# Softmax attention with a gated MLP on one core: head quads outside, chunks inside, VectorE exponentials as four shifted bit lines, one shifted add on GpSimd

## Chip, cores, metric

One core of one Trainium2 chip. The metric is device time in microseconds (us) of one execution. On one core the state of a run (fast or slow) is judged only by its time against other runs of the same kernel. Ratios below are of fast runs, made on the same chip side by side with the kernel before; times are medians of all runs. Experiments of different rounds ran on different chips, on which the kernel before took 1037.57 to 1041.86 us. "Quarter" means 512 of the 2048 columns of one batch; a "batch" is one key block of 128 keys for four heads and 512 queries, exponentiated on VectorE.

## The reference

```python
x = A_x                                    # 1 x 2048 x 640, bf16
g = sigmoid((x * gate_w).sum(-1, keepdims=True))
q, k, v = split(x @ wqkv)                  # 32 heads of 20 dimensions
p = softmax(q @ k.T * 20 ** -0.5)          # 2048 x 2048 for each head
a = (p @ v) @ wo
h = x @ w1 + b1                            # 640 -> 1536
b = (h * tanh(log1p(exp(-|h|)) + max(h, 0))) @ w2
return g * a + (1 - g) * b
```

There are 32 x 2048 x 2048 exponentials. They are the heavy part: 32 groups (four heads by 512 queries), each with 16 key blocks.

## The kernel before

A scheduler written in Python lays all work in one fixed order per engine when the program is built. It uses assumed costs (in ns); each engine is then given its instructions in that order. TensorE computes scores into PSUM, ScalarE exponentiates 13 of 16 key blocks in tiles of 1536 and 1024 columns, VectorE the other three, and TensorE multiplies by V ("PV"), accumulating a group in one PSUM bank, `C`. VectorE's exponential writes integers whose bits, read as bf16, are close to an exponential (a "bit line"), and mends it with a mantissa polynomial:

```python
DVE_KEYS = (6, 10, 14)                  # the other 13 key blocks are ScalarE's
...
def p1(r=r, db=db, vb_=vb_):            # one bit line of 512 columns, from PSUM
    nc.vector.tensor_scalar(out=vb_.tile[:, r * QC:(r + 1) * QC], in0=db.tile[:, :],
        scalar1=P * LOG2E * inv, scalar2=127.0 * P, op0=ALU.mult, op1=ALU.add)
...
# then, for 4 heads x 512 columns: two bit operations (n, m) of 2048 columns,
# two squares and two products of 1024 columns each, all on VectorE
pv_four(G, j, 1, sl(vb_), list(p1s), [vb_], key=G)      # three PV sets a key block
pv_four(G, j, 0, sl(nb_), [tn], [nb_], key=G)
pv_four(G, j, 2, sl(mb_), tp_, [mb_], key=G)
```

A PV set is four matmuls, one for each head, each on 32 of the 128 columns of the array. The projections (K, Q, MLP, output) are whole 128-column matmuls, put between. GpSimd only clears and pads buffers at the start.

The softmax here doesn't subtract the row's maximum and nothing guards it: scores larger than these inputs give would overflow.

Of the kernel before, what the change touches and what calls it, by code (L numbers as in the profile page):

```python
# [2 lines left out]

# [9 lines left out]
ENG = mybir.EngineType  # L13
# [9 lines left out]
VW = 22  # L23
NO = 12


DVE_KEYS = (6, 10, 14)
ACT_KEYS = tuple(j for j in range(NS) if j not in DVE_KEYS)



COEF = (0.458054, 0.465699, 0.0762946)
SCALE = 0.5 / COEF[1]
COEF = tuple(SCALE * c for c in COEF)
LOG2E = 1.4426950408889634


class Task:
    __slots__ = (
        "eng", "cost", "fn", "deps", "after", "prio", "ring", "need", "frees",  # L40
        "start", "end", "lat", "mode", "rows", "n", "key", "left", "succ",
    )

    def __init__(self, eng, cost, fn, deps=(), after=None, prio=5, ring=None,
                 frees=(), lat=70, mode=None, rows=(), key=0):
        self.eng, self.cost, self.fn = eng, cost, fn
        self.deps, self.after, self.prio = [d for d in deps if d], after, prio
        self.ring, self.frees = ring, list(frees)
        self.lat, self.mode, self.rows, self.key = lat, mode, rows, key
        self.start = self.end = None  # L50


class Ring:
    def __init__(self, *slots):
        self.free = deque((0.0, s) for s in slots)

    def when(self):
        return self.free[0][0] if self.free else None


class Buf:


    def __init__(self, ring):
        self.ring, self.users, self.tile, self.last, self.slot = ring, 0, None, 0.0, None


class Order:


    SWITCH = 60.0
# [10 lines left out]

    def run(self):
        now = {}
        mode = None
        rows = set()
        open_ = {}
        waiting = {}
        for i, t in enumerate(self.tasks):
            t.n = i  # L90
            t.succ = []
            t.left = 0
        for t in self.tasks:
            for d in set(t.deps + ([t.after] if t.after else [])):
                d.succ.append(t)
                t.left += 1
            open_.setdefault(t.eng, [])
            now.setdefault(t.eng, 0.0)
            if t.left == 0:
                open_[t.eng].append(t)  # L100
        done = 0
        out = []
        self.rowheld = 0

        def est(t):
            e = now[t.eng]
            for d in t.deps:
                ready = d.end + (d.lat if d.eng != t.eng else 0 if t.eng == "PE" else 40)
                if ready > e:
                    e = ready  # L110
            if t.after and t.after.start > e:
                e = t.after.start
            if t.ring:
                w = t.ring.ring.when()
                if w is None:
                    return None
                e = max(e, w + 70)
            return e

        def cost(t):  # L120
            if t.eng != "PE":
                return t.cost
            c = t.cost
            if t.mode != mode:
                c += self.SWITCH
            elif t.mode == "row" and not (rows & set(t.rows)):
                c = 40
            return c

        while done < len(self.tasks):  # L130
            best = None
            for eng, lst in open_.items():
                c = [(est(t), t) for t in lst]
                c = [(e, t) for e, t in c if e is not None]
                if not c:
                    continue
                first = min(e for e, _ in c)
                pick = None
                if eng == "PE":
                    hot = [(e, t) for e, t in c if t.prio == 0]  # L140
                    lim, ht = min(hot, key=lambda x: x[0], default=(1e12, None))
                    slack = 0 if ht is None else 350 if len(ht.rows) == 3 else 750
                    here = [(e, t) for e, t in c if e <= first + 1]
                    if any(t.mode == "row" and t.prio == 1 for _, t in c) and not self.rowheld:
                        here = [
                            (e, t) for e, t in here
                            if not (t.ring and t.prio > 1 and len(t.ring.ring.free) < 2)
                        ]
                    here.sort(key=lambda x: (x[1].prio, x[1].key, x[1].n))
                    for e, t in here:  # L150
                        if t.mode == "row" and t.prio == 1 and lim < 1e12 and not (
                            mode == "row" and not (rows & set(t.rows))
                        ):
                            continue
                        if t.prio == 0 or e + cost(t) <= lim + slack:
                            pick = (e, t)
                            break
                    if pick is None:
                        pick = min(hot or c, key=lambda x: x[0])
                    if mode == "row" and pick[1].prio != 0:  # L160
                        for e, t in here:
                            if t.mode == "row" and t.prio == 1 and not (rows & set(t.rows)):
                                pick = (e, t)
                                break
                else:
                    here = [(e, t) for e, t in c if e <= first + 20]
                    pick = min(here, key=lambda x: (x[1].prio, x[1].key, x[1].n))
# [3 lines left out]
            c = cost(t)  # L171
            if t.eng == "PE":
                if t.mode == "row" and mode == "row" and not (rows & set(t.rows)):
                    rows |= set(t.rows)
                else:
                    rows = set(t.rows)
                mode = t.mode
            t.start, t.end = e, e + c
            now[t.eng] = t.start + (60 if t.eng == "SP" else c)
            open_[t.eng].remove(t)  # L180
            if t.mode == "row" and t.prio == 1:
                self.rowheld += 1
            if t.ring:
                t.ring.slot = t.ring.ring.free.popleft()[1]
            if t.eng == "DVE" and t.prio == 1 and t.rows:
                self.rowheld -= 1
            for b in t.frees:
                b.users -= 1
                b.last = max(b.last, t.end)
                if b.users == 0:  # L190
                    f = b.ring.free
                    f.append((b.last, b.slot))
                    b.ring.free = deque(sorted(f))
            for s in t.succ:
                s.left -= 1
                if s.left == 0:
                    open_[s.eng].append(s)
            done += 1
# [5 lines left out]
ORDER = []  # L204


def vcost(n, per=1.04, base=160):
    return base + per * n
# [3 lines left out]
def kernel(  # L212
# [11 lines left out]
):  # L224
    nc = tc.nc
# [3 lines left out]
    use_dve = len(DVE_KEYS) > 0  # L229
    NA, ND = len(ACT_KEYS), len(DVE_KEYS)  # L230

    const = ctx.enter_context(tc.tile_pool(name="const", bufs=1))
    ident = const.tile([P, P], BF16, tag="ident")
    kt_all = const.tile([P, NP, S], BF16, tag="kt_all")
    xt = const.tile([P, NQ, KT, QC], BF16, tag="xt")
    va = const.tile([P, NA * H * VW + 16], BF16, tag="va")
    vd = const.tile([P, max(1, 3 * ND) * H * VW + 16], BF16, tag="vd", name="vd")
    wq = const.tile([P, NP, KT, P], BF16, tag="wq")
    wo = const.tile([P, NP, D], BF16, tag="wo")
    w1 = const.tile([P, KT, F], BF16, tag="w1")  # L240
    w2k = const.tile([P, 5120 + KT * 641 + 3], BF16, tag="w2k")
# [4 lines left out]
    z = const.tile([P, NS], F32, tag="z")  # L246
    lnc = const.tile([P, 1], F32, tag="lnc")
    arena = const.tile([P, 18432], BF16, tag="arena")

    w2 = w2k[:, 0:FT * D].rearrange("p (f c) -> p f c", c=D)  # L250
    wk = w2k[:, 0:NP * KT * P].rearrange("p (q k c) -> p q k c", q=NP, k=KT)
    wv = w2k[:, 5120:5120 + KT * 641].rearrange("p (k c) -> p k c", c=641)
    xs = arena[:, 0:NS * D].rearrange("p (s c) -> p s c", c=D)
    wqk = arena[:, 10240:10240 + KT * 2 * D].rearrange("p (k c) -> p k c", c=2 * D)
    hs = arena[:, 0:FT * QC].rearrange("p (f q) -> p f q", q=QC)
    tanh_in = arena[:, 6144:6144 + FT * QC].rearrange("p (f q) -> p f q", q=QC)
    outs = arena[:, 6144:6144 + NU * D].rearrange("p (u c) -> p u c", c=D)
    otn = arena[:, 12288:12288 + NO * QC].rearrange("p (h q) -> p h q", q=QC)
    bs = xt[:, 0].rearrange("p k q -> p (k q)").rearrange("p (u c) -> p u c", c=D)

    psum = ctx.enter_context(tc.tile_pool(name="psum", bufs=1, space=bass.MemoryType.PSUM))
    epool = ctx.enter_context(tc.tile_pool(name="epool", bufs=3))
    vpool = ctx.enter_context(tc.tile_pool(name="vpool", bufs=2))
    qpool = ctx.enter_context(tc.tile_pool(name="qpool", bufs=3))
    opool = ctx.enter_context(tc.tile_pool(name="opool", bufs=1))
    spool = ctx.enter_context(tc.tile_pool(name="spool", bufs=2))
# [4 lines left out]
    R = {  # L271
        "S3": Ring(0), "S2": Ring(0), "X": Ring(0, 1), "E3": Ring(0, 1, 2), "E2": Ring(0, 1),
# [568 lines left out]
```

## Time and profile before

1043.57 us (median of 3, 1031.25 to 1044.37).

| what | before |
|---|---|
| span of the profiled run | 1038.2 us |
| ScalarE (ACT) busy | 921.6 us, 89% |
| TensorE (PE) busy | 831.3 us, 80% |
| VectorE (DVE) busy | 790.8 us, 76% |
| GpSimd (POOL) busy | 35.3 us, 3% |
| mean granted TensorE clock | 0.859 |

The page's first part of the kernel before: busy us of each engine, its share of the span, instructions. Then the first line of the page's fourth part: the chain of work that ended last, shares of the span.

```profile
PE 831.3 (80%) x6247; PEld 267.3 (26%) x6304; DVE 790.8 (76%) x1322; ACT 921.6 (89%) x731; POOL 35.3 (3%) x29
...
ACT 49%; PE 28%; issue 11%; DVE 7%; DMA 4%; SPq 1%; ACTq 0%; DVEq 0%
```

ScalarE is the busiest engine and holds half of the chain: it is what the change must relieve.

Groups of instructions by shape, of the kernel before. Columns: line, engine, operation, out<-in, shapes, count | busy us, mean ns of one | idle us of the engine before them and who ended it.

```profile
L597 ACT ACTIVATE E<-S,lnc 128x1536 bf16<-128x1536 f32 x333 | 523.0, 1571 | 27.7 <-PE S L579 19.3 <-PE X L634 8.2
L597 ACT ACTIVATE E<-S,lnc 128x1024 bf16<-128x1024 f32 x332 | 379.9, 1144 | 44.8 <-PE C L507 41.9 <-PE X L634 1.5 <-PE S L579 0.6
...
L646 DVE TENSOR_SCALAR e<-X 128x512 uint16<-128x512 f32 x384 | 260.8, 687 | 135.7 <-PE X L634 131.8 <-PE S L579 1.1
...
L653 DVE TENSOR_SCALAR n<-e 128x2048 uint16<-128x2048 uint16 x96 | 65.8, 685 | 0.0
...
L328 POOL COPY wq<-arena 128x400 bf16<-128x400 bf16 x7 | 3.4, 523 | 0.0
```

The last line is one of two alike, the only elementwise work for which GpSimd reads a tile in this trace, apart from one 0.3 us instruction that builds the identity matrix: a bf16 copy of 400 columns. Remember it. No line shows GpSimd adding to a uint16 tile.

Two stretches of the table of stretches, kernel before (us from the start: length, then busy us and instruction count of each engine, then the granted TensorE clock, DMA share and GB/s):

```profile
416.00:442.00 26.00, 25.47 (x220) 9.73 (x220) 23.47 (x41) 25.48 (x21) 0.00 (x0) 1.00 0.09 31
...
494.00:520.00 26.00, 16.05 (x103) 4.30 (x105) 18.68 (x28) 24.31 (x18) 0.00 (x0) 0.75 0.05 11
```

ScalarE (the fourth busy figure) is near 26 of 26 us in both. In the first TensorE was busy for 25.47 us and its clock was 1.00; in the second for 16.05 us, at 0.75.

### The profile page before, as it was taken

The numbers are of one execution on the slowest core, as the hardware profiler recorded it, in microseconds if no ns is written. First come the engines' busy times: TensorE is split into PE (matmuls) and PEld (weight loads), VectorE is DVE, ScalarE is ACT, GpSimd is POOL, SyncE is SP. The second block draws the span as 40 slices with busy tenths as digits, with TensorE's granted clock in tenths as the row PEclk, the third lists the DMA queues.
The fourth block names the chain that finished last, engine by engine and source line by source line (L and its number), as shares of the span: only waits on it lengthen the run. The fifth ranks groups of instructions, "written<-read, shape, count | busy, mean of one in ns | idle before, by whom it ended". The sixth has DMA issues, their size and how long they took to land.

```text
span 1038.2 us, 15472 instructions
## 1 busy us (share of the span) xinstructions
PE 831.3 (80%) x6247; PEld 267.3 (26%) x6304; DVE 790.8 (76%) x1322; ACT 921.6 (89%) x731; POOL 35.3 (3%) x29
## 2 busy tenths in 40 slices
PE   2899988887886589996689889667988967798885
PEld 1432222221121123321123322112322311132213
DVE  1698989887784769995679879677888975689772
ACT  1757879998999999999999999999999999999991
POOL 9300000000000000000000000000000000000000
PEclk9998999886696779997789989787989997599766
DMA  7400000011000000000000000000000000000001
GB/s 196 109 1 12 12 11 11 12 55 36 9 12 11 11 1 12 25 24 12 11 1 12 18 25 18 12 12 1 12 12 25 24 12 11 1 12 12 11 11 37
DMA packets 28495, 22.36 MB, mean 22 GB/s; under 512 B 15496, under 2 KB 23688, under 8 KB 28424
## 3 DMA queue, kind: packets, MB, share of 16 engines
q1 hardware_dynamic: 24744, 19.15, 6.7%
q10 hardware_dynamic: 3680, 2.23, 0.8%
q8 instruction: 49, 0.80, 0.3%
q14 instruction: 22, 0.18, 0.1%
HBM read 18.22 MB, written 2.88 MB: 20 GB/s over the span
## 4 chain that ended last, share of the span: by engine, by line
ACT 49%; PE 28%; issue 11%; DVE 7%; DMA 4%; SPq 1%; ACTq 0%; DVEq 0%
ACT E L597 40%; PE S L579 8%; PE C L507 7%; ACT arena L745 6%; PE X L763 3%; PE X L778 3%; PE X L427 2%; DVE e L646 2%; ACT L745 2%; PE X L439 2%; DMA rbc<-rows 2%; PE X L462 2%; PE X L727 1%; DMA w2k<-in_A_wqkv_dram 1%; ACT L597 1%
## 5 line engine op out<-in xcount | busy, mean ns | idle before, releaser
L597 ACT ACTIVATE E<-S,lnc 128x1536 bf16<-128x1536 f32 (+1 forms) x666 | 822.4, 1357 | 72.5 <-PE C L507 41.9
L579 PE MATMUL S<-q,kt_all 32*128 32x512 bf16 x1664 | 290.5, 428 | 146.1 <-ACT E L597 139.7
L646 DVE TENSOR_SCALAR e<-X 128x512 uint16<-128x512 f32 x384 | 260.8, 687 | 135.7 <-PE X L634 131.8
L507 PE MATMUL C<-E,va 128*32 128x512 bf16 x1664 | 183.3, 438 | 2.7 <-DVE oraw L690 1.5
L579 PEld LDWEIGHTS <-kt_all 32*128 32x128 bf16 x1664 | 83.4, 92 | 382.7 <-issue 375.6
L634 PE MATMUL X<-q,kt_all 32*128 32x512 bf16 x384 | 156.1, 428 | 3.6 <-DVE e L646 3.3
L663 DVE TENSOR_TENSOR m<-m 128x1024 bf16<-128x1024 bf16 x192 | 127.2, 683 | 0.3
L668 DVE TENSOR_TENSOR m<-m,e 128x1024 bf16<-128x1024 bf16 x192 | 126.6, 681 | 0.0
L507 PEld LDWEIGHTS <-va 128*32 128x32 bf16 x1664 | 42.5, 95 | 129.4 <-issue 127.4
L727 PE MATMUL X<-xt,w 128*128 128x512 bf16 x219 | 70.5, 416 | 2.5 <-issue 1.7
L658 DVE TENSOR_SCALAR m<-e 128x2048 uint16<-128x2048 uint16 x96 | 66.2, 690 | 6.6 <-PE C L507 4.0
L763 PE MATMUL X<-w2k,arena 128*128 128x320 bf16 x384 | 69.6, 305 | 0.7 <-DVE e L646 0.7
L745 ACT ACTIVATE arena<-arena 128x2048 bf16<-128x2048 bf16 x36 | 68.2, 1917 | 0.2
L653 DVE TENSOR_SCALAR n<-e 128x2048 uint16<-128x2048 uint16 x96 | 65.8, 685 | 0.0
L778 PE MATMUL X<-wo,arena 128*128 128x320 bf16 x256 | 49.3, 325 | 7.8 <-DVE arena L717 6.5
L507 PE MATMUL C<-e,vd 128*32 128x512 bf16 x384 | 49.5, 442 | 4.1 <-DVE e L646 2.2
L507 PE MATMUL C<-m,vd 128*32 128x512 bf16 x384 | 49.1, 452 | 4.2 <-DVE m L668 4.2
L439 PE MATMUL X<-xt,wq 128*128 128x512 bf16 x137 | 48.6, 446 | 2.3 <-issue 1.8
L733 DVE TENSOR_SCALAR arena<-X,b 128x512 bf16<-128x512 f32 x48 | 35.8, 746 | 18.7 <-PE X L727 18.5
L507 PEld LDWEIGHTS <-vd 128*32 128x32 bf16 x1152 | 34.6, 99 | 57.7 <-issue 51.6
L507 PE MATMUL C<-n,vd 128*32 128x512 bf16 x384 | 42.7, 432 | 5.7 <-DVE n L653 5.5
L427 PE MATMUL X<-xt,w2k 128*128 128x512 bf16 x147 | 44.2, 403 | 2.4 <-issue 1.1
(55 smaller groups left out, 435.7 us busy)
## 6 DMA issues: line engine op xcount, KB each, us to landing
rbc<-rows SPq DMA_DIRECT2D x128, 64.0 KB
out_dram<-arena SPq DMA_DIRECT2D x16, 160.0 KB
w<-in_B_w_dram SPq DMA_DIRECT2D x1, 1920.0 KB
w2k<-in_B_w_dram SPq DMA_DIRECT2D x1, 1920.0 KB
arena<-in_A_wqkv_dram SPq DMA_DIRECT2D x2, 700.0 KB
arena<-in_A_x_dram ACTq DMA_DIRECT2D x2, 640.0 KB
arena<-in_A_x_dram SPq DMA_DIRECT2D x2, 640.0 KB
wo<-in_A_wo_dram SPq DMA_DIRECT2D x4, 200.0 KB
```

What stands on the lines that cost most here:

```text
L439: nc.tensor.matmul(t[:, 0:QC], lhsT=wq[:, p, k, :], rhs=xt[:, qc, k, :], start=a, stop=b)
L507: nc.tensor.matmul(acc[32 * r:32 * r + 32, :], lhsT=ten[:, off:off + 32], rhs=srcs[r](), start=k == 0, stop=k == pv_per - 1, tile_position ...
L579: nc.tensor.matmul(sb.tile[:, a * QC:(a + 1) * QC], lhsT=kt_all[32 * r:32 * r + 32, G % NP, j * P:(j + 1) * P], rhs=q_buf[G].tile[32 * r:3 ...
L597: nc.scalar.activation(eb.tile[:, 0:w], sb.tile[:, 0:w], ACT.Exp, bias=lnc, scale=inv)
L634: nc.tensor.matmul(db.tile[:, :], lhsT=kt_all[32 * r:32 * r + 32, G % NP, j * P:(j + 1) * P], rhs=q_buf[G].tile[32 * r:32 * r + 32, :], st ...
L646: nc.vector.tensor_scalar(out=vb_.tile[:, r * QC:(r + 1) * QC], in0=db.tile[:, :], scalar1=P * LOG2E * inv, scalar2=127.0 * P, op0=ALU.mul ...
L663: nc.vector.tensor_tensor(out=m, in0=m, in1=m, op=ALU.mult)
L668: nc.vector.tensor_tensor(out=m, in0=m, in1=e, op=ALU.mult)
L727: nc.tensor.matmul(t[:, 0:QC], lhsT=w1[:, k, ft * P:(ft + 1) * P], rhs=xt[:, c, k, :], start=a, stop=b)
L745: nc.scalar.activation(v, hs[:, 4 * a:4 * a + 4, :] if func == ACT.Exp else v, func, bias=1.0 if func == ACT.Ln else 0.0)
L763: nc.tensor.matmul(t[:, 0:320], lhsT=hs[:, k, u * P:(u + 1) * P], rhs=w2[:, k, 320 * hf:320 * hf + 320], start=a, stop=b)
L778: nc.tensor.matmul(t[:, 0:320], lhsT=otn[:, (c * NP + k) % NO, u * P:(u + 1) * P], rhs=wo[:, k, 320 * hf:320 * hf + 320], start=a, stop=b)
```

## The change

Intent: take more exponentials off ScalarE and make VectorE's cheaper. Four of 16 key blocks go to VectorE. Each is now a sum of four bit lines: the first is made from PSUM as before, three are the same integers plus 19, 51 and 90; the sum is made by PV's accumulation, so a key block has four PV sets instead of three and no polynomial. Two of the three shifted adds are VectorE's, the third is GpSimd's, in quarters. The loops are turned round: four heads outside, the four query chunks inside, so K and V are projected a bit at a time through the whole run. The projections (V's excepted) become four 32-column matmuls ("column-tiled"), so that TensorE need not change mode between them and PV. The mode is the way the array is divided for a matmul: whole, in strips of columns or in strips of rows; the scheduler reckons 100 ns for a change. Mish loads fewer activation tables (9 loads instead of 25).

The core of the diff:

```diff
-DVE_KEYS = (6, 10, 14)
-COEF = (0.458054, 0.465699, 0.0762946)
+SHIFTS = (0, 19, 51, 90)
+SUM = 5.2566
+def dve_keys(G):
+    n = 4
+    return [int((i + 0.4) * NS / n) for i in range(n)]
+TB = (2, 2, 1, 1)                      # buffers of each line's tile
+SHIFT_ON = {1: ("DVE", 1), 2: ("DVE", 1), 3: ("POOL", 4)}
 ...
+    def columns(t, width, lhsT, rhs, a, b):
+        for r in range(4):
+            nc.tensor.matmul(t[32 * r:32 * r + 32, 0:width], lhsT=lhsT(r), rhs=rhs,
+                             start=a, stop=b, tile_position=(0, 32 * r))
 ...
-            # bit operations n, m; squares; products (VectorE)
+        for i in range(1, len(SHIFTS)):
+            eng, parts = SHIFT_ON[i]
+            now = []
+            for a in range(parts):
+                def add(i=i, eng=eng, a=a, w=4 * QC // parts):
+                    ...
+                    (nc.vector if eng == "DVE" else nc.gpsimd).tensor_scalar(
+                        out=bufs[i].tile[:, a * w:(a + 1) * w],
+                        in0=bufs[0].tile[:, a * w:(a + 1) * w],
+                        scalar1=float(SHIFTS[i]), scalar2=None, op0=ALU.add)
+                n = 4 * QC // parts
+                now.append(o.add(eng, 150 + 0.264 * n if eng == "DVE" else 160 + 1.0 * n, add,
+                                 p1s[...] + now[-1:], prio=3, ...,
+                                 rings=[bufs[i]] if a == 0 else [], frees=[bufs[0]], port=True))
 ...
-        qc, p = divmod(G, NP)
+        p, qc = divmod(G, NQ)
```

(Cut: the scheduler's rewritten choice rules, new loads, the placing of the normalized output.) Note the assumed cost of a GpSimd quarter, `160 + 1.0 * n` = 672 ns, and `port=True`: the scheduler plans VectorE's shifted adds and GpSimd's quarters as excluding each other.

## The prediction

> **Bound now: ScalarE.** The page's first part has ACT busy 921.6 us of 1038.2 (89%), PE 831 (80%), DVE 791 (76%), GpSimd 35. In the chain of waits ACT's exponential line holds 40%. By the table of stretches ACT runs at about 97% from 286 to 1014 us. Its 117 us of idle time: 27 us before the first exponential, 24 us after the last, about 30 us between 52 and 156 us, where the K and V projections of all heads crowd.
>
> **ScalarE after.** VectorE takes four of 16 key blocks instead of three: 1536 exponential blocks for 1664, 307 pairs (1536 and 1024 wide) for 332.5. Their union is 834 us for 665, 2.51 us a pair (neighbours overlap): -64 us. The new instruction order has 9 activation table loads for 25, each 1.28 us: up to -20 us. ACT busy about 850 us.
>
> **VectorE after.** Out: 192 bit operations (0.69 us), 384 half-tile multiplies (0.68 us), threefold V copies: about -400 us. In: 128 more bit lines from PSUM (0.69 us, +88) and 256 shifted adds of 2048 columns (estimate 0.69 us, as the bit operations: +177). In all about 735 us. GpSimd gets 512 quarter adds; its copy of 400 columns took 524 ns, so I estimate 0.67 us each, 345 us. The Trainium skill, "SBUF — State Buffer", section "Who interferes with whom", says that a DVE instruction in a 2-port mode and a GpSimd instruction exclude each other for a whole instruction; the trace before has no such overlap. I allow 30 to 60 us of lengthened adds: DVE busy 765 to 795 us.
>
> **TensorE after.** PV goes from 22 to 28 sets of four matmuls per group (+192 x 0.21 = +41 us at full clock); output projection 8 to 6 steps (-9 us). Projections become four column-tiled matmuls, which cost one slot as PV fours do (0.21 to 0.23 us apart in the timeline) and need no mode change against PV: in the instruction order mode changes fall from about 1500 to 1250, at about 0.1 us (-25 us). TensorE's work stays equal within 10 us. Stretches with denser PE had clock 1.00, the thinner Mish ones 0.72 to 0.83; spread work should hold 0.85 to 0.95.
>
> **Head quads outside** spreads K and V projections over the run: most of the 30 us of early idle time goes. The start loads less before the first exponential (27 us to about 20). The tail gains a placing DMA but loses matmul time: about 24 us again.
>
> **Sum.** ACT 850 + start 20 + tail 25 + inner idle 30 to 60 (DVE gets denser) = 925 to 955. Predicted 938 us, range 905 to 985. Chances: faster by over 2% 0.92, within 2% 0.06, slower 0.02.
>
> **What would show it.** ACT busy 840 to 865 and leader of the chain; 615 exponentials; 9 table loads; DVE 765 to 795, shifted adds over 0.69 us on average; GpSimd 320 to 400; no ACT stretch after 60 us under 90%; PE busy share 80 to 88%.
>
> **What would make it wrong.** GpSimd's quarters much longer than 0.67 us, so that the lock makes DVE the bound (over 88% busy) and ScalarE waits for PE, PE for VectorE's bit lines; column-tiled projections of 320 columns over 0.14 us a slot because four weight loads do not hide; a lower TensorE clock: towards 985 or beyond. A start and steady stretch without gaps: towards 905.

## The result and the profile after

1111.22 us (median of 4, 1106.65 to 1114.51) against 1041.86 us: the ratio of the fast runs is 1.068, 95% interval 1.060 to 1.077. (Ratios here and below are the mean time of one kernel's fast runs over that of the other's in the same rounds, so not quite the ratio of the quoted medians.) The change is slower by 7%, outside the range and on the wrong side.

The same two parts of the page, of the changed kernel:

```profile
PE 945.5 (85%) x10616; PEld 307.2 (28%) x10616; DVE 721.5 (65%) x1097; ACT 853.1 (77%) x663; POOL 837.1 (75%) x519
...
PE 42%; POOL 38%; DVE 7%; ACT 7%; issue 5%; DMA 1%; SPq 0%; DVEq 0%; ACTq 0%; POOLq 0%
```

ScalarE did fall to the 850 us that were predicted, yet the run got longer: it is now idle for 257 us (1110.2 - 853.1). GpSimd is busy for 837 us instead of the predicted 345, and holds 38% of the chain.

Groups by shape, changed kernel:

```profile
L674 POOL TENSOR_SCALAR t<-t 128x512 uint16<-128x512 uint16 x512 | 831.5, 1643 | 244.5 <-PE C L588 123.0 <-DVE t L661 117.3 <-PE X L407 3.7
L627 ACT ACTIVATE E<-S,lnc 128x1536 bf16<-128x1536 f32 x307 | 473.7, 1543 | 176.8 <-PE C L588 113.1 <-PE X L600 34.2 <-PE S L600 27.0
...
L674 DVE TENSOR_SCALAR t<-t 128x2048 uint16<-128x2048 uint16 x256 | 211.2, 833 | 11.3 <-PE C L588 9.3
```

A quarter takes 1643 ns on average, 2.4 times what the scheduler assumed and I estimated. The query of that source line gives the spread (min/median/max ns, first and last start in us):

```profile
L674 POOL TENSOR_SCALAR t<-t x512: 1482/1490/2467, 17.8 to 1080.5; 128x512 uint16<-128x512 uint16 x171
L674 DVE TENSOR_SCALAR t<-t x256: 629/738/1148, 22.5 to 1081.0; 128x2048 uint16<-128x2048 uint16 x128
```

The minimum and the median are alike: 1.49 us is what the instruction costs when nothing disturbs it. The 0.15 us up to the mean are taking turns with VectorE (experiment 6, where they vanish).

Who waited for whom, changed kernel (us in total, times, longest us):

```profile
ACT E L627 <- PE C L588: 133.8, 113, 6.4
...
POOL t L674 <- PE C L588: 123.0, 108, 9.4
POOL t L674 <- DVE t L661: 117.3, 87, 11.7
...
PE C L588 <- POOL t L674: 85.0, 98, 2.0
```

And how this looks in time: the timeline of the changed kernel, GpSimd's, ScalarE's and some of TensorE's rows of PV on bit lines.

```profile
524.39 6.84 POOL L674 TENSOR_SCALAR t<-t 128x512 uint16<-128x512 uint16 x4 [2.13 <-PE C L588]
...
528.94 0.39 PE L588 MATMUL C<-t,va 128*32 128x512 bf16 x2
...
529.83 0.38 PE L588 MATMUL C<-t,va 128*32 128x512 bf16 x1 [0.50 <-POOL t L674]
...
531.28 0.38 PE L588 MATMUL C<-t,va 128*32 128x512 bf16 x1 [1.08 <-POOL t L674]
...
531.74 5.86 POOL L674 TENSOR_SCALAR t<-t 128x512 uint16<-128x512 uint16 x4 [0.51 <-PE C L588]
...
532.31 4.18 ACT L627 ACTIVATE E<-S,lnc 128x1536 bf16<-128x1536 f32 x3 [1.77 <-PE S L600]
...
536.20 0.38 PE L588 MATMUL C<-t,va 128*32 128x512 bf16 x1 [0.93 <-POOL t L674]
...
537.65 0.58 PE L588 MATMUL C<-t,va 128*32 128x512 bf16 x1 [1.08 <-POOL t L674]
...
538.32 1.49 POOL L674 TENSOR_SCALAR t<-t 128x512 uint16<-128x512 uint16 x1 [0.72 <-PE C L588]
```

This is a loop. GpSimd makes four quarters (about 6.5 us). TensorE's PV set on this line stands in its queue early, as the plan wanted, and its four matmuls wait one by one for the quarters; nothing behind them runs meanwhile (from 529.83 to 531.28 us TensorE starts no other matmul), so no scores reach ScalarE. Only when the last is through is the line's single buffer free, and GpSimd starts the next batch. From the first quarter to the last this takes (1080.5 - 17.8 - 3 x 1.64) / 127 = 8.3 us a batch; 128 batches are 1066 us.

### The profile page after: what moved, and what is told of

Its sections match the earlier page's. It is cut to its first block, busy times and chain, and to the rows that moved or that the text cites. A ratio compares the mean times of both kernels' runs of the same rounds, so it can differ in the third digit from the quotient of the medians.

```text
span 1110.2 us, 24877 instructions
## 1 busy us (share of the span) xinstructions
PE 945.5 (85%) x10616; PEld 307.2 (28%) x10616; DVE 721.5 (65%) x1097; ACT 853.1 (77%) x663; POOL 837.1 (75%) x519
## 3 DMA queue, kind: packets, MB, share of 16 engines
HBM read 18.47 MB, written 2.89 MB: 19 GB/s over the span
## 4 chain that ended last, share of the span: by engine, by line
PE 42%; POOL 38%; DVE 7%; ACT 7%; issue 5%; DMA 1%; SPq 0%; DVEq 0%; ACTq 0%; POOLq 0%
POOL t L674 38%; PE C L588 15%; PE S L600 10%; PE X L407 8%; ACT E L627 5%; DVE t L661 4%; PE X L600 2%; PE X L479 2%; PE X L462 2%; PE X L498 2%; DVE t L674 1%; ACT arena L771 1%; DVE arena L757 1%; PE X L369 0%; DMA arena<-in_A_x_dram 0%
## 5 line engine op out<-in xcount | busy, mean ns | idle before, releaser
L674 POOL TENSOR_SCALAR t<-t 128x512 uint16<-128x512 uint16 x512 | 831.5, 1643 | 244.5 <-PE C L588 123.0
L627 ACT ACTIVATE E<-S,lnc 128x1536 bf16<-128x1536 f32 x615 | 777.6, 1328 | 217.9 <-PE C L588 133.8
L661 DVE TENSOR_SCALAR t<-X 128x512 uint16<-128x512 f32 x512 | 347.2, 687 | 263.6 <-PE X L600 246.3
L588 PE MATMUL C<-t,va 128*32 128x512 bf16 x2048 | 265.0, 441 | 92.3 <-POOL t L674 85.0
L600 PE MATMUL S<-q,kt 20*128 20x512 bf16 x1536 | 272.4, 438 | 35.5 <-ACT E L627 34.1
L674 DVE TENSOR_SCALAR t<-t 128x2048 uint16<-128x2048 uint16 x256 | 211.2, 833 | 11.3 <-PE C L588 9.3
L600 PE MATMUL X<-q,kt 20*128 20x512 bf16 x512 | 209.6, 435 | 7.3 <-DVE t L661 5.2
L407 PE MATMUL X<-w,arena 128*32 128x320 bf16 x1536 | 84.3, 320 | 3.0 <-DVE t L661 1.6
L407 PE MATMUL X<-xt,w 128*32 128x512 bf16 x960 | 82.3, 403 | 4.8 <-DVE arena L757 1.9
L479 PE MATMUL X<-xt,wqk 128*32 128x512 bf16 x560 | 55.0, 437 | 1.0 <-DVE t L661 0.7
L462 PE MATMUL X<-xt,wqk 128*32 128x512 bf16 x560 | 49.7, 428 | 1.5 <-DVE t L661 1.1
```

The costliest lines, as they stand in the source:

```text
L407: nc.tensor.matmul(t[32 * r:32 * r + 32, 0:width], lhsT=lhsT(r), rhs=rhs, start=a, stop=b, tile_position=(0, 32 * r))
L462: nc.tensor.matmul(t[32 * r:32 * r + 32, 0:QC], lhsT=w, rhs=xt[:, sc, k, :], start=k == 0, stop=k == KT - 1, tile_position=(0, 32 * r))
L479: nc.tensor.matmul(t[32 * r:32 * r + 32, 0:QC], lhsT=w, rhs=xt[:, qc, k, :], start=k == 0, stop=k == KT - 1, tile_position=(0, 32 * r))
L588: nc.tensor.matmul(acc[G][32 * r:32 * r + 32, :], lhsT=va4[:, (p // 2) % 2, j, h * VW:h * VW + 32], rhs=buf.tile.bitcast(BF16)[:, off * QC ...
L600: nc.tensor.matmul(t[:, off * QC:(off + 1) * QC], lhsT=kt[32 * r:32 * r + DH, (p % 2) * S + j * P:(p % 2) * S + (j + 1) * P], rhs=q_buf[G] ...
L627: nc.scalar.activation(eb.tile[:, 0:w * QC], sb.tile[:, 0:w * QC], ACT.Exp, bias=lnc, scale=inv)
```

## The experiments

Theory A: GpSimd's add is slow, and its loop (four quarters, PV, release) became the longest thing per batch. Rivals: B, the turned loops and TensorE's column-tiled and extra matmuls overload TensorE; C, the plan's order is at fault, as it was laid for 672 ns; D, the port's mutual exclusion, not GpSimd's own pace; E, the single buffer. Twelve kernels were measured, and one more did not build (experiment 7); all times are medians, ratios are to the kernel before in the same rounds.

### 1. The third add on VectorE

```diff
-SHIFT_ON = {1: ("DVE", 1), 2: ("DVE", 1), 3: ("POOL", 4)}
+SHIFT_ON = {1: ("DVE", 1), 2: ("DVE", 1), 3: ("DVE", 1)}
```

> The only edit: the third shifted add (shift 90) is made by VectorE in one instruction of 2048 columns, not by GpSimd in quarters; everything else of the change stays, the static order being worked out anew. Theory A (GpSimd's add is the fault: 1490 ns for a quarter where the order assumes 672 ns, so that PV matmuls stand in TensorE's in-order queue ahead of their data): 920 to 975 us, ScalarE busy 845 to 860 and back over 88% of the span, VectorE busy 760 to 790 (721 less about 35 us of lock waits plus 128 x 0.69). Rival B (head quads outside, column-tiled projections and the six further PV sets per group overload TensorE, 945 us busy in the changed kernel): over 1060 us, TensorE still over 900 us busy and half-clock stretches as before.

Measured: correct, 942.92 us, ratio 0.909 (0.903 to 0.915), inside A's range (the busy times of ScalarE, 841.7 us, and VectorE, 754.9 us, are a little under theirs). The page's first part, and the chain's first line, of this kernel, then the group of its shifted adds:

```profile
PE 853.5 (91%) x10616; PEld 306.5 (33%) x10616; DVE 754.9 (80%) x1225; ACT 841.7 (90%) x663; POOL 5.5 (1%) x7
...
PE 58%; ACT 22%; DVE 10%; issue 6%; DMA 2%; SPq 1%; ACTq 0%; DVEq 0%
```

```profile
L674 DVE TENSOR_SCALAR t<-t 128x2048 uint16<-128x2048 uint16 x384 | 252.1, 682 | 3.3 <-PE C L588 1.6
```

One dictionary entry turns 7% slower into 9% faster. Rival B falls: the same 10616 matmuls took 945.5 us busy in the changed kernel and 853.5 us here. TensorE's extra busy time was an effect: in the changed kernel it waits, its mean clock is 0.837, here it is 0.896. (The order moved too; with the changed kernel's own order and a cheaper add on GpSimd, experiment 3, it is busy for 860.1 us.) VectorE makes the whole third line of a batch in 0.68 us; GpSimd needed 6.5 us. VectorE has the room: 80% busy.

### 2. Telling the scheduler the true cost

```diff
-... else 160 + 1.0 * n, add,
+... else 1640, add,
```

> The only edit: the cost that the scheduler assumes for a GpSimd quarter is 1640 ns, as measured, instead of 672 ns; the work is the same, only the static order moves. If the loss is the order (PV placed ahead of its data), 980 to 1030 us and the 85 us for which TensorE waited for GpSimd fall under 30. If the loss is GpSimd's pace with one buffer for its result (a batch of 4 x 1.64 us, then PV, then the next), 1060 to 1120 us whatever the order.

> As the true-cost kernel, and GpSimd's result has two buffers instead of one (the room is found by laying the first weight columns into a part of the arena that is unused at the start). If the serial loop through the single buffer is what limits (GpSimd idle for 123 us waiting for PV to release it), 20 to 60 us faster than the true-cost kernel, GpSimd's idle time on PV under 40 us. If not, within 1% of it.

(The second of these also sets `TB = (2, 2, 1, 2)` and lays `w0` into an unused part of `arena`, to find 2 KB.)

Measured: 1213.79 us (ratio 1.171) with the true cost alone, and 1190.82 us (1.147) with the second buffer too. The first is worse than any expectation I had written; the second buffer is worth 23 us of it, as expected, and cuts GpSimd's wait for PV from 348.9 to 2.9 us; a wait of 339.5 us for VectorE's bit lines takes its place. The honest order does cut TensorE's waits for GpSimd (the quarters' 85.0 us become 18.4 and 1.5 us), but ScalarE then waits 267.1 and 254.0 us for PV to release its buffers. The scheduler's own plan, which is only the sum of its assumed costs and no measurement, ended at 912 us for the changed kernel and ends at 1155 and 1140 us here: with exclusion and 1640 ns it found no short order. (The 1640 ns already hold 150 ns of turns at the port, which the plan then adds once more; 1490 ns was not tried.) So rival C falls as a remedy with this scheduler, which does worse when told the truth. That no order suits a slow quarter is not shown. Why its true-cost order loses a further 100 us was not taken apart.

### 3. A cheaper add on GpSimd, in the same order

Two uint16 values are added as one 32-bit integer; the result stays exact, as there is no carry between the halves.

```diff
+    c90 = const.tile([P, QC // 2], I32, tag="c90")     # 90 in both halves
 ...
+    nc.gpsimd.tensor_tensor(
+        out=bufs[i].tile.bitcast(I32)[:, a * w // 2:(a + 1) * w // 2],
+        in0=bufs[0].tile.bitcast(I32)[:, a * w // 2:(a + 1) * w // 2],
+        in1=c90, op=ALU.add)
```

> GpSimd adds two 16-bit lines at a time: a tensor-tensor add of 32-bit integers with a constant tile of 90 in both halves, 256 words a quarter instead of 512 half-words. The result should be exact (no carry between the halves). If GpSimd's cost goes with the number of elements, a quarter falls from 1.49 us to between 0.5 and 0.9 us, and the kernel comes to 925 to 985 us in the order that assumed 0.67 us. If a two-input integer add is slower per element than 2.9 ns, a quarter stays near 1.5 us and the time near 1110 us.

> As the int32 kernel (951 us), with the same static order, but GpSimd makes every packed add twice (the result is the same). GpSimd's time per quarter goes from 0.87 us to about 1.74 us (1.45 us without lock waits), as in the changed kernel. If GpSimd's pace alone makes the loss: 1080 to 1150 us. If the loss has to do with the uint16 form of the add, or with anything else that the int32 kernel changed: under 1000 us.

> A dose between the int32 kernel (once: four quarters at 0.87 us, 951 us) and the one with every add made twice (1151 us): quarters 0 and 2 are made twice, 1 and 3 once, same static order. GpSimd's batch takes about 5.2 us, with the wait for PV near 7 us, about the 7 us that a batch has in a run of 950 us. If the loss appears only once GpSimd's loop is the longest: 960 to 1010 us. If the loss grows evenly with GpSimd's time: about 1050 us.

"Twice" repeats the add (`for _ in range(2)`), "half twice" repeats it for quarters 0 and 2 (`range(2 - a % 2)`). The instruction order of TensorE, ScalarE and VectorE is the same in all three and in the changed kernel, so of the work only GpSimd's add differs, in form and time. All results are correct. The three times lie in the ranges for A or for a loss that starts late, "twice" a hair past the edge (1150.61 for 1080 to 1150 us). GpSimd's lines of the kernels with the add once, half of them twice, and all twice:

```profile
L678 POOL TENSOR_TENSOR t<-t,c 128x256 int32<-128x256 int32 x512 | 439.9, 872 | 480.6 <-DVE t L664 275.6 <-PE C L591 191.4 <-PE X L410 6.8
```

```profile
L679 POOL TENSOR_TENSOR t<-t,c 128x256 int32<-128x256 int32 x768 | 632.5, 838 | 334.4 <-PE C L591 165.7 <-DVE t L664 140.2 <-PE X L410 4.5
```

```profile
L679 POOL TENSOR_TENSOR t<-t,c 128x256 int32<-128x256 int32 x1024 | 837.5, 830 | 275.9 <-PE C L591 113.2 <-DVE t L664 110.8 <-DVE arena L794 7.5
```

| kernel, same order on the other engines | GpSimd us per batch (busy / 128) | time us | ratio |
|---|---|---|---|
| int32, once | 439.9 / 128 = 3.4 | 951.06 | 0.917 |
| int32, half of them twice | 632.5 / 128 = 4.9 | 995.76 | 0.958 |
| the change, uint16 | 831.5 / 128 = 6.5 | 1111.22 | 1.068 |
| int32, twice | 837.5 / 128 = 6.5 | 1150.61 | 1.109 |

This is the strongest evidence for A: with every other engine's order held fixed, a cheap GpSimd add gives 951 us and doubling that add alone gives the loss back. It also bends: the first 1.5 us per batch cost 45 us of run, the next 1.6 us cost 115 to 155 us (if all of it were on the chain, 1.6 us x 128 = 205 us). The bend is soft, not a threshold. At equal GpSimd time the doubled kernel is 40 us slower than the change; VectorE's shifted adds were longer there (899 against 833 ns), but I did not test that this is the reason.

### 4. A second buffer in the original order

`TB = (2, 2, 1, 2)`, with `w0` laid into the arena; the scheduler sees the second buffer, so its order moves too.

> The changed kernel with two buffers for GpSimd's result instead of one, and with the scheduler's cost left at 672 ns. If the serial loop through one buffer (four quarters, PV, release, next four) sets the pace, the batch period falls from 8.3 us towards the 6.6 us that four quarters take: 960 to 1040 us. If GpSimd's own pace and TensorE's order bind already, 1080 to 1110 us.

Measured: 1041.44 us, ratio 1.004 (1.000 to 1.009), just above the first range; the batch period is (1011.5 - 16.7 - 3 x 1.67) / 127 = 7.8 us. GpSimd's line of this kernel:

```profile
L674 POOL TENSOR_SCALAR t<-t 128x512 uint16<-128x512 uint16 x512 | 841.9, 1665 | 165.6 <-DVE t L661 160.6 <-PE C L588 2.5
```

GpSimd's wait for PV falls from 123 to 2.5 us and 70 of the 168 us between the change and the 943 us kernel are gone. Rival E is thus a part: the single buffer made GpSimd's slow add serial with PV. The rest stays. A likely reason, not tested by itself, is that 6.6 us of GpSimd per batch hardly fit into the 7 us that a batch has in a run of 943 us (912.5 us of shifted adds, less the start at 19.6 us, by 128).

### 5. GpSimd makes half the line

Quarters 0 and 1 on GpSimd, the other 1024 columns in one VectorE instruction (`SHIFT_ON[3] = ("MIX", 4)`, three parts).

> GpSimd makes two quarters of the third add (uint16 as in the change, 1.49 us each), VectorE the other half in one instruction of 1024 columns[...]. GpSimd busy near 400 us. If pace is the cause: 930 to 965 us, with GpSimd still in use and still taking turns with VectorE at the port. If any use of GpSimd beside VectorE's shifted adds costs: well over 1000 us.

Measured: correct, 966.30 us, ratio 0.931 (0.926 to 0.936): GpSimd busy 420 us. Just above the expected range, and on A's side: using GpSimd is not what makes the loss, though this is 23 us slower than the kernel with no add on GpSimd.

### 6. No VectorE add that could exclude GpSimd

```diff
             eng, parts = SHIFT_ON[i]
+            if i < 3:                    # wrong on purpose: lines 1 and 2 are line 0
+                made.append(p1s)
+                continue
 ...
-            ... bufs[i], r) for r in range(4)])
+            ... bufs[0 if i < 3 else 3], r) for r in range(4)])
```

> Wrong result on purpose: VectorE's two shifted adds are taken out and PV reads the unshifted line in their place, so TensorE's work stays, GpSimd's 512 quarters stay, and VectorE makes no instruction that could exclude GpSimd in the loop. If GpSimd's own 1.49 us sets the pace: quarters flat at 1.49 us, 1040 to 1100 us. If exclusion between VectorE's adds and GpSimd makes the loss: 940 to 980 us.

Measured: 1096.33 us, ratio 1.055 (1.049 to 1.062); the result is wrong (relative error 0.034). GpSimd's line:

```profile
L677 POOL TENSOR_SCALAR t<-t 128x512 uint16<-128x512 uint16 x512 | 756.4, 1498 | 301.5 <-PE C L588 180.8 <-DVE t L661 102.6 <-DVE arena L787 16.5
```

The quarters are flat at 1498 ns, so nothing disturbs them, and the run is still 59 us slower than the kernel before beside it (1037.57 us). Rival D is worth about 15 us of time here (1111 - 1096), not the loss. This is rough: the edit also takes VectorE's work for 256 adds away, and the scheduler laid a new order. Exclusion is real but small: per instruction it added 145 ns to a quarter (1643 - 1498) and 151 ns to a VectorE add (833 - 682).

### 7. Looking for a better version

With the third add on VectorE, TensorE is 91% busy.

```diff
-    n = 4
+    n = 3            # or: 4 - G % 2
```

> The best kernel so far (third shifted add on VectorE, 943 us) with three of 16 key blocks on VectorE instead of four, as the kernel before had. ScalarE gets 128 blocks more (+64 us of busy time, to about 906 us), TensorE loses 96 PV sets (-20 us at full clock), VectorE about 175 us. If ScalarE then binds as in the kernel before: 960 to 990 us, and the fourth key block is worth 2 to 5%. If TensorE is the bound at four key blocks (91% busy): no worse than 945 us.

> Third shifted add on VectorE, and four and three VectorE key blocks in turn, group by group. If ScalarE and TensorE are in balance at four blocks, 945 to 965 us, between the kernels with four and with three; below 940 us only if TensorE alone binds at four.

> The int32 kernel (951 us) with two buffers for GpSimd's result (the constant shrunk to 8 words read over and over, so that it fits; the same kernel did not fit with the full constant). VectorE is relieved of 88 us against the 943 us kernel, GpSimd's loop is short (3.5 us of 7 us). If TensorE binds there: 938 to 952 us, no gain that matters over the 943 us kernel. If the single buffer still cost something at 951 us: 920 to 938 us, the best of all.

Measured: three key blocks 1009.77 us (ratio 0.970; one of four runs counts as slow, the fast ones have the median 1008.9), four and three in turn 999.81 us (0.954; two of four runs count as slow, the fast ones took 983.99 and 998.6). Both miss my ranges on the slow side, in fast runs by 19 us and by 19 to 34 us. So the fourth key block is worth about 65 us. Neither reading of the first expectation holds: were TensorE alone the bound at four blocks, three should not have been slower. In the kernel with three, ScalarE is busy for 906 us as expected and idle for 100 us (1006.9 - 906.2) of a span of 1006.9 us, the chain is TensorE's for 46%, and the clock is 0.829 against 0.896. That a less dense TensorE got a lower clock fits, but whether the clock or the order is the cause stays open.

Int32 adds with two buffers: 948.33 us, ratio 0.909 (0.905 to 0.914), the same as the third add on VectorE. GpSimd waits for PV for 4.1 us in all there, and nothing is gained. TensorE is busy for 90% and holds 62% of the chain; that it alone binds is not shown, as the kernel with three key blocks speaks against it. The version to keep is the one-entry edit of experiment 1: 943 us, as fast as any and simpler.

## Why the prediction was wrong, point by point

**The step that failed**, in its own words: "GpSimd gets 512 quarter adds; its copy of 400 columns took 524 ns, so I estimate 0.67 us each, 345 us." Measured: 1.49 us undisturbed, 1.64 us on average, 831.5 us in all. A bf16 copy is not a uint16 tensor-scalar add. The scheduler's own cost, 672 ns, agreed with my estimate, and I took that as support; it was no measurement. The prediction named this failure ("GpSimd's quarters much longer than 0.67 us") but gave slower than before a chance of 0.02, and sized its effect as "towards 985": it looked for the damage in VectorE's busy time. It came by another way: the slow quarters themselves, a single buffer, a PV set that waits in TensorE's in-order queue, and scores stuck behind it. VectorE was less busy than predicted (721.5 us, not 765 to 795).

**Of the rest, most held.** With that one term put right by moving the add (experiment 1), the kernel takes 943 us; the sum had said 938. Nearer still to the prediction's own kernel is the int32 one (experiment 3): the same order, a quarter of 0.73 us undisturbed, 951 us. Part of this agreement is luck: the sum runs along ScalarE, but in experiment 1 TensorE holds 58% of the chain and ScalarE 22%. In detail:

- ScalarE "about 850 us": 853.1; 615 exponentials and 9 table loads: as counted.
- Exclusion, "30 to 60 us of lengthened adds": 256 x (833 - 682) ns = 39 us. The Trainium skill ("SBUF — State Buffer") was the right warning, of the smaller effect.
- VectorE "in all about 735 us": the terms listed give 790.8 - 400 + 88 + 177 = 656 us; measured, without the 39 us of lengthening, 682 us.
- Column-tiled projections "cost one slot": in the changed kernel 12 matmuls of 320 columns take 0.58 us and 24 take 0.99, so a set of four takes (0.99 - 0.58) / 3 = 0.137 us. The four weight loads do hide.
- TensorE "80 to 88%": 85%, but for the wrong reason, and 91% in the kernel of experiment 1, where it leads the chain. "Equal within 10 us" is not borne out there: 853.5 us busy at a mean clock of 0.896, before 831.3 us at 0.859. Busy time by clock, a rough estimate, is 765 against 714 us. Which of its terms (PV, mode changes, projections) was off was not taken apart. The clock "0.85 to 0.95": 0.837 in the changed kernel, 0.896 in experiment 1.
- The start: the first exponential began at 13.3 us instead of 27.4, earlier than the 20 predicted, but after four of them ScalarE waited 8.7 us for the next scores.
- "No ACT stretch after 60 us under 90%" was the test that failed plainly: most stretches of 26 us in the changed kernel show 18 to 23 us. In experiment 1 the stretches from 52 to 156 us have 104 - 47.84 - 48.20 = 8 us of idle time, against 104 - 13.63 - 18.47 - 22.93 - 18.94 = 30 us before, as was predicted of turning the loops; no run tests that edit alone.

## What to carry to other kernels

An engine's instruction that no trace has timed (this operation, this element type, this engine) is the term to measure first; neither a neighbouring instruction nor a cost written into the kernel replaces it. Before moving work to an idle engine, compare its time per round, with the wait for its buffer to come free, to the period of the round: here 6.5 us plus a release against 7 us. On engines that run in a fixed order, a late producer with one buffer stopped here everything queued behind its consumer, so the loss appeared on other engines, as ScalarE's and TensorE's waits, and GpSimd, with a busy share of 75%, already set the pace.

## What the Trainium skill lacked or had wrong

- "GPSIMD Engine Reference", section 3.1, gives about 1.8 cycles an element as the best case of a tight loop (512 elements in 769 ns), and section 4.1 calls one-input operations "roughly line-rate". Here a uint16 tensor-scalar add of 512 columns took 1490 ns, about 3.5 cycles an element at the page's 1.2 GHz (an estimate from the two figures, the fixed cost of an instruction included). VectorE made 2048 columns of it in 682 ns, GpSimd in 4 x 1490 ns: 8.7 times slower, where the page has about 2 times for two-input operations. A 32-bit integer tensor-tensor add of 256 elements took 727 ns in the median, about 3.4 cycles an element (fixed cost again included), where the page has 2.6 for a two-input float add. A cost of the built-in operations by element type is missing.
- The same page's "Exact integer add" (section 4.1) held: two packed uint16 values added as one int32 gave correct results in four kernels, at half the cost of the uint16 add (727 against 1490 ns a quarter).
- "SBUF — State Buffer", section "Who interferes with whom", says that the one which starts second blocks fully until the other ends. For the int32 adds the trace agrees (1 of the 96 VectorE adds that began inside a quarter ended before it). For the uint16 quarters it does not: of the 217 VectorE adds that began inside a quarter in the changed kernel, 135 ended before that quarter did, by about 463 ns. (The profile's page calls spans on GpSimd rough, so this is what the records say and no proof.) The timeline of the changed kernel, GpSimd and VectorE, shows one, of undisturbed length and wholly inside a quarter that grew from 1.49 to 1.64 us:

```profile
75.95 1.64 POOL L674 TENSOR_SCALAR t<-t 128x512 uint16<-128x512 uint16 x1 [0.45 <-DVE t L661]
76.44 0.68 DVE L674 TENSOR_SCALAR t<-t 128x2048 uint16<-128x2048 uint16 x1
```

- "TensorEngine Tiling (Array Packing)" says in its restrictions that column tiling disables fast weight loads and gives no cost; four column-tiled matmuls of 320 columns, with their four weight loads, took 0.137 us a set in a row here.
